# Attention and two MLPs on one core: four sequences per attention turn, and a planner that takes VectorE and GpSimd as excluding each other

## The chip, the cores and the metric

The kernel runs on one core of a Trainium2 chip. Its time is the device time of one execution in microseconds (us); the three timed runs of the kernel before gave 564.5, 564.63 and 563.31 us, median 564.5. The engines are named as the profile names them: PE (TensorE; PEld is its weight load), DVE (VectorE), ACT (ScalarE), POOL (GpSimd), SP (SyncE, which here issues every DMA).

## What is computed

Three layers stand one behind the other. The first is a linear attention with decay, in chunks of the sequence (4 sequences, 8 heads, 768 positions, head width 32, state width 16); the other two are MLPs over the 3072 rows of 256 values that it makes (inner width 2048).

```python
for c in range(nc):                                   # chunks, in order
    cum = np.cumsum(la, axis=-1)                      # la = log of the decay a
    L = np.exp(cum[..., :, None] - cum[..., None, :]) * causal
    M = np.einsum('bhin,bhjn->bhij', Cc, Bc) * L
    y_intra = np.einsum('bhij,bhjd->bhid', M, xc)
    y_inter = np.einsum('bhin,bhnd->bhid', Cc, state) * np.exp(cum)[..., None]
    y[:, :, sl] = y_intra + y_inter
    state = decay_full * state + np.sum(Bx, axis=2)   # Bx: B and x, decayed to the chunk's end
x = softplus(y_rows @ w_in) @ w_out                   # first MLP
x = g2(x @ w2_in) @ w2_out                            # second MLP; g2 is 0, a square, or the value itself
```

## The kernel before

**Work units.** A chunk is 128 positions, so there are NC = 6 chunks of four sequences (NB = 4), and a *unit* u is one sequence in one chunk (u = 4c + b). The 512 columns of a chunk (4 sequences by 128 positions) are what the MLPs take at a time. An MLP *step* is one slice of 128 inner values for one chunk: `up` (6 matmuls of 512 columns into a PSUM bank `h`, L1262 to L1264), the activation on ACT, its split into a rounded half `g_hi` and a rest `g_lo`, and `down` (6 matmuls into the chunk's two accumulators `acc`, L1398). Each MLP has 16 steps a chunk. Later chunks and the second MLP form pairs of chunks in products with fewer multiplications (L1269 to L1271). At the start some steps are cut: a half step has 256 columns (two sequences) and two slices. The first `WHOLE` steps take `down` in one product of full precision (L1386) in place of three rounded ones, and so need no rounded weights of the second kind.

**Attention.** Chunk 0 goes unit by unit. From chunk 1 on a *pair* of units goes through three PE jobs, each with MLP steps between: `scores` (L1104), the products of B and C, into four PSUM banks (the pair `y` and two of the four `acc`); `st` (L1172, L1150), half of the intra-chunk product and the new states into `y`; and `out` (L1204, L1172), the rest. Between `scores` and `st` DVE multiplies the scores by the decays (`weigh`, L1118, into `ld`); between `st` and `out` it updates the state (`carry`, L1160) and ACT masks it (`sm`, L1241). Behind `out` ACT takes the sums out of PSUM (`evac`) and DVE makes the rest (`ready`, L1232). The decays of a pair come from DRAM into one of two `ld` buffers (`rows`, L1039; DVE then scans them, L1069), x, B and C into one of four `u` buffers (L1028); both are given back by `out`.

**Order.** `program` lists all jobs with their needs, engines, costs and buffers, and `Jobs.order` (L47) simulates the engines with these costs and picks the next job by due time. The order so found is written out engine by engine, and each engine keeps to it. Where a DVE and a POOL job overlap, the planner lengthens both by factors from the table `SHARED` (L495); `RUSH` (L526) moves single due times; jobs with two engines in braces go to the one that ends first by the plan. Where the plan leaves PE idle in the first 26 us, matmuls without use (`idle`, L1477) are put in.

Of the kernel before, what the change touches and what calls it, by code (L numbers as in the profile page):

```python
# [27 lines left out]
class Jobs:  # L28
# [18 lines left out]
    def order(self, slots, begin):  # L47
# [33 lines left out]
        busy = {DVE: [], POOL: []}  # L81
# [19 lines left out]
        for _ in range(len(jobs)):  # L101
            best = []
            for name in ready:
# [11 lines left out]
                (b for b in best if b[4] == first[4] and b[0] <= first[0] + (PATIENCE if first[0] > EARLY else HASTE)), key=lambda b: (b[1], b[0], b[2])  # L115
# [8 lines left out]
            if engine in (DVE, POOL):  # L124

                kind = name if isinstance(name, str) else name[0]
                other = POOL if engine == DVE else DVE
                for a, b, k in busy[other][-3:]:
                    shared = max(0.0, min(b, start + cost) - max(a, start))
                    cost += shared * SHARED[engine].get(kind, 0.0) * (k > 0)  # L130
                    if b == clock[other]:
                        clock[other] += shared * k * (SHARED[engine].get(kind, 0.0) > 0)
                busy[engine].append((start, start + cost, SHARED[engine].get(kind, 0.0)))
# [63 lines left out]

def pair_of(u):

    return u | 1  # L200
# [12 lines left out]
def program():  # L213
# [27 lines left out]
    for hg in range(2):  # L241
        add(("columns", hg), DVE, 610, needs=["terms"] + [("rows_of", 0)] * hg)
    for b in range(NB):
        add(("rows_of", b), DVE, 210, needs=["terms"] + [("columns", 1), ("rows_of", b - 1)] * (b == NB - 1), gives=["terms"] * (b == NB - 1))
# [7 lines left out]
    for u in range(NU):  # L252
# [18 lines left out]
        if c == 0:  # L271
            for hg in range(2):
                add(
                    ("sources", u, hg), POOL, 400, takes=["bt"] * (hg == 0),
                    needs=[("load", u), ("decay", u, hg)] + ([("sources", u, 0)] if hg else []),
                )
        else:
            add(("sources", u), DVE, 210, needs=[("load", u)] + decay, takes=["bt"])
        if b % 2:
            v = u // 2  # L280
            add(
                ("scores", v), PE, 830 if c else 1270, needs=[("load_bc", v)] + (decay + [("decay", u - 1)] if c else [("scores", v - 1)] * v),
                takes=["y", "y", "acc", "acc"] if c else ["y", "y"] + [("acc", "h")] * 2 if v == 0 else [("h", "acc")] * 4,
                gives=[("load_bc", v)],
            )
        for hg in range(2):
# [3 lines left out]
            bank = [("part", ("scores", u // 2), b % 2 * 2 + hg)]  # L290
            if n in WEIGH_POOL:
                add(("copy", u, hg), ACT, 490, needs=[("scores", u // 2)], takes=["g"], gives=bank)
                add(("weigh", u, hg), POOL, 1350, needs=weighed + [("copy", u, hg)], gives=[("copy", u, hg)])
            else:
                add(("weigh", u, hg), DVE, 340 if c else 600, needs=weighed + [("weigh", u, 0)] * hg + [("scores", u // 2)], gives=bank)
        both = [u] if c == 0 else [u - 1, u]
        if c == 0 or b % 2:

            needs = [("weigh", i, hg) for i in both for hg in range(2)] + ([("out", both[0] - 1)] if u else [])
            if c > 0:  # L300
                add(
                    ("st", u), PE, 990, needs=needs + [("sm", u - NB)], takes=["y", "y"], gives=[("sources", i) for i in both],
                )
                add(("carry", u), DVE, 300, needs=[("st", u), ("dec", c)])
                add(("sm", u, 1), ACT, 500, needs=[("carry", u)])
                needs = [("st", u), ("sm", u, 1)] + [("cd", i) for i in both]
# [5 lines left out]
            needs = [("out", u)]  # L312
# [3 lines left out]
            if c == 1:  # L316

                needs += [("w2" if signed(0, kind, SX) else "w3", 0, kind, SX) for kind in "io"]
            due = when(first_step[c, b] - LEAD if c < 2 else min(first_step[c, b] - LEAD, CHUNK * (c - 1) + SPACE * b + SHIFT))
# [3 lines left out]
                gives=[("st", u) if c else ("out", u)] + [("dec", c)] * (b == NB - 1 and c > 0),  # L323
# [13 lines left out]
    for m in range(2):  # L337
        for j in sorted(range(8), key=lambda j: first_use[m, j]):
            for kind in "io":
# [20 lines left out]
                if m == 0:  # L360
                    add(("split_w", *w), {DVE: 610, POOL: 1500}, needs=[("w_hi", *w)])
# [44 lines left out]
    for s, (m, c, t0, n, fc, m_fc) in enumerate(steps):  # L406
# [47 lines left out]
        else:  # L454
            add(("g_hi", s), {ACT: 520, DVE: 360}, needs=[("g", s)], takes=["gh"])
            add(("g_lo", s), {DVE: 610, POOL: 1500} if s < GL_POOL else {DVE: 610}, needs=[("g_hi", s)], takes=["gl"], gives=[("g", s)])
# [8 lines left out]
        if s == same[-1]:  # L465
            root = ("down", same[0])
            for e in range(2):
                own = when(s) + LAG + 2000 if m else None
                add(("finish_hi", s, e), {ACT: 490, DVE: 610}, due=own, needs=[("down", s)],
                    takes=[("w32", "cs")] * (m + (s == len(steps) - 1 and e)), gives=[("part", root, e)] * m)  # L470
# [7 lines left out]
    slots = dict(sx=2, h=2, y=2, z=0, acc=4, t=2, g=N_G, gh=4, gl=3, ld=3, lp=2, u=4, bc=3, bt=3, dec=2, st=2, st2=1, st3=1, w32=5, cs=2)  # L478
# [1052 lines left out]
```

## Time and profile before

| what | value |
|---|---|
| timed runs | 564.5, 564.63, 563.31 us (median 564.5) |
| the profiled execution: its own time | 563.84 us |
| its span in the profile | 561.9 us |
| time outside the span | 1.94 us |
| PE busy | 553.3 us, 98% |
| DVE, ACT, POOL busy | 449.9, 385.1, 27.6 us |
| granted TensorE clock, mean | 0.998 |

The profile gives each instruction's start and duration. A matmul of 512 columns is recorded as some 0.39 us long, but the next one starts after some 0.23 us, since they are pipelined; how long a step of PE takes is therefore read from start to start. Within a view of instructions in order of time equal neighbours are merged (x32), and a bracket tells the idle time ahead and what ended it.

### The profile page before, as it was taken

To read this page: it belongs to the slowest core of one execution; us is meant where nothing else is said; L and a number is where in the kernel's file an instruction comes from. 1 tells how busy PE (TensorE), PEld (TensorE's weight loads), DVE (VectorE), ACT (ScalarE), POOL (GpSimd) and SP (SyncE) were. 2 spreads that over 40 slices of the span, in tenths; PEclk is the share of its full clock that TensorE was granted. 3 is DMA by queue.
4 is the path that set the end of the run, shared out by engine and by line. 5 is a ranking of instruction groups with operands and counts; after the bars stand their busy time and mean duration, and the time that the engine had idled before them with its cause. 6 is when DMAs were issued, how large, how long until landed. Compare 5 with 4: busy or idle time off the path is not lost.

```text
span 561.9 us, 10574 instructions
## 1 busy us (share of the span) xinstructions
PE 553.3 (98%) x4070; PEld 445.4 (79%) x4070; DVE 449.9 (80%) x841; ACT 385.1 (69%) x706; POOL 27.6 (5%) x34
## 2 busy tenths in 40 slices
PE   9899999999999999999999999999999999999997
PEld 4767898777778888788888788788788888888885
DVE  6899976687896899877897999967976665876664
ACT  6977744445555666756657887886787785777873
POOL 4030300000000100000100000200100000000000
PEclk9999999999999999999999999999999999999999
DMA  8986541658445003578847132103200001000002
GB/s 283 389 225 187 157 118 31 196 171 225 119 149 178 0 2 93 214 237 304 275 142 240 59 118 90 56 6 108 76 0 1 0 1 38 37 1 0 1 1 76
DMA packets 34679, 64.74 MB, mean 115 GB/s; under 512 B 3684, under 2 KB 8164, under 8 KB 34628
## 3 DMA queue, kind: packets, MB, share of 16 engines
q1 hardware_dynamic: 34628, 64.06, 35.3%
q8 instruction: 32, 0.52, 0.4%
q14 instruction: 19, 0.16, 0.1%
HBM read 47.61 MB, written 16.43 MB: 114 GB/s over the span
## 4 chain that ended last, share of the span: by engine, by line
PE 91%; DVE 4%; DMA 2%; ACT 1%; SPq 1%; issue 1%; DVEq 0%; ACTq 0%
PE acc L1398 44%; PE h L1262 5%; PE h L1269 4%; PE h L1263 4%; PE h L1264 4%; PE h L1271 4%; PE h L1270 4%; PE z L1269 4%; PE z L1271 4%; PE z L1270 4%; PE y L1172 2%; DMA st<-in_w_out_dram 2%; PE acc L1386 1%; PE y L1204 1%; PE y L1104 1%
## 5 line engine op out<-in xcount | busy, mean ns | idle before, releaser
L1372 DVE TENSOR_TENSOR gl<-g,gh 128x512 fp32r<-128x512 f32 x184 | 126.5, 692 | 51.3 <-PE acc L1398 35.4
L1398 PE MATMUL acc<-gh,woh 128*128 128x512 f32 (+1 forms) x384 | 148.9, 390 | 0.0
L1398 PE MATMUL acc<-gh,wol 128*128 128x512 f32 (+1 forms) x384 | 146.5, 384 | 0.0
L683 ACT CAST gh<-g 128x512 fp32r<-128x512 f32 x155 | 96.1, 620 | 32.2 <-PE acc L1398 18.4
L1398 PE MATMUL acc<-gl,woh 128*128 128x512 f32 (+1 forms) x384 | 115.1, 383 | 0.0
L1398 PEld LDWEIGHTS acc<-gh,woh 128*128 128x128 f32 x384 | 72.1, 188 | 16.1 <-issue 1.2
L1398 PEld LDWEIGHTS acc<-gh,wol 128*128 128x128 f32 x384 | 72.2, 188 | 13.5 <-DVE wol L916 0.2
L1398 PEld LDWEIGHTS acc<-gl,woh 128*128 128x128 f32 x384 | 70.9, 188 | 14.4
L1357 ACT ACTIVATE g<-h 128x512 f32<-128x512 f32 x65 | 38.7, 595 | 56.2 <-PE h L1264 41.3
L1349 ACT ACTIVATE t<-t 128x512 f32<-128x512 f32 x96 | 60.8, 634 | 1.9
L1262 PE MATMUL h<-xh,wih 128*128 128x512 f32 (+1 forms) x130 | 48.5, 373 | 0.0
L1263 PE MATMUL h<-xh,wil 128*128 128x512 f32 (+1 forms) x130 | 46.6, 358 | 0.7 <-DVE wil L916 0.7
L1264 PE MATMUL h<-xl,wih 128*128 128x512 f32 (+1 forms) x130 | 46.3, 356 | 0.0
L1263 PEld LDWEIGHTS h<-xh,wil 128*128 128x128 f32 x130 | 24.5, 189 | 4.8 <-DVE wil L916 1.1
L1069 DVE TENSOR_TENSOR_SCAN ld<-ld,eye_t 128x512 f32<-128x512 f32 x20 | 25.8, 1326 | 3.2 <-DMA ld<-clip_z 3.2
L1262 PEld LDWEIGHTS h<-xh,wih 128*128 128x128 f32 x130 | 24.5, 189 | 4.5 <-issue 0.4
L1264 PEld LDWEIGHTS h<-xl,wih 128*128 128x128 f32 x130 | 24.5, 189 | 3.6
L1342 ACT ACTIVATE t<-h 128x512 f32<-128x512 f32 x37 | 22.1, 597 | 7.6 <-PE h L1271 6.0
L1361 DVE TENSOR_TENSOR g<-h,t 128x512 f32<-128x512 f32 x37 | 25.3, 684 | 1.8 <-ACT t L1349 0.8
L1361 DVE TENSOR_TENSOR g<-z,t 128x512 f32<-128x512 f32 x35 | 23.8, 683 | 1.5 <-ACT t L1349 0.8
L1342 ACT ACTIVATE t<-z 128x512 f32<-128x512 f32 x35 | 20.9, 596 | 5.5 <-PE z L1271 3.2
L1322 DVE TENSOR_TENSOR dec_plain<-h,dec_plain 128x512 f32<-128x512 f32 x22 | 15.1, 688 | 7.8 <-PE h L1271 7.6
(321 smaller groups left out, 1004.2 us busy)
## 6 DMA issues: line engine op xcount, KB each, us to landing
st<-in_w_in_dram SPq DMA_DIRECT2D x15, 512.0 KB, 4.0
st<-in_w_out_dram SPq DMA_DIRECT2D x15, 512.0 KB, 4.2
u<-in_ub_dram SPq DMA_DIRECT2D x24, 256.0 KB, 5.5
ld<-clip_z SPq DMA_DIRECT2D x20, 256.0 KB, 4.6
bc<-in_bc_dram SPq DMA_DIRECT2D x12, 384.0 KB, 7.9
pre_i<-st_plain SPq DMA_DIRECT2D x14, 256.0 KB, 3.6
pre_o<-st_plain SPq DMA_DIRECT2D x12, 256.0 KB, 3.7
pre_s<-st_plain SPq DMA_DIRECT2D x14, 192.0 KB, 4.0
```

The source lines that it names most:

```text
L683: nc.scalar.copy(out, in_)
L1262: nc.tensor.matmul(o, wh, xh[c][:, k, t0:t0 + n], start=(k == 0), stop=False)
L1263: nc.tensor.matmul(o, wl, xh[c][:, k, t0:t0 + n], start=False, stop=False)
L1264: nc.tensor.matmul(o, wh, xl[c][:, k, t0:t0 + n], start=False, stop=(k == 1))
L1269: nc.tensor.matmul(bank, wh, bh, start=start, stop=False, skip_group_check=True)
L1270: nc.tensor.matmul(bank, wl, bh, start=False, stop=False, skip_group_check=True)
L1271: nc.tensor.matmul(bank, wh, bl, start=False, stop=True, skip_group_check=True)
L1342: nc.scalar.activation(out=t, in_=ph, func=act_funcs.IDENTITY_SAT240, scale=SAT)
L1349: nc.scalar.activation(out=t, in_=t, func=AF.Square, scale=0.5 / SAT, bias=0.5)
L1361: nc.vector.tensor_tensor(out=g, in0=ph, in1=t, op=ALU.max)
L1372: engines[engine].tensor_tensor(out=mine("g_lo", s)[0], in0=mine("g", s)[0], in1=mine("g_hi", s)[0].bitcast(F32), op=ALU.subtract)
L1398: nc.tensor.matmul(acc_t(s, e), w, g[:, j * n:(j + 1) * n], start=(begins(e, j) and g is gh and i == 0), stop=(fc + j == NFC - 1 and g is ...
```

## The change

Four things change. (1) In chunks 1 to 5 (`TOGETHER`) the three PE jobs each take all four units; the states then go to two `acc` banks, the four units' sums fill the pair `y`, the first two units' scores stand in the first half of a bank and the others' in the second, and `u`, `ld` and `bt` are given back by one `out` for all. (2) The planner: a POOL job starts where no DVE job of the set `LOCKED` runs, and such a DVE job waits for the end of a POOL job that has begun; constants and due times differ, `SHARED` is gone and `RUSH` is short; chunk 1 has no half steps, and 8 steps, not 6, take the full-precision `down`. (3) `rows_of`, four products that fill the rows of exponents for chunk 0, may run on ACT. (4) Of the last result, which two engines copy out in halves, ACT issues the first half's transfer.

```diff
-            if engine in (DVE, POOL):
-
-                kind = name if isinstance(name, str) else name[0]
-                other = POOL if engine == DVE else DVE
-                for a, b, k in busy[other][-3:]:
...
+            kind = name if isinstance(name, str) else name[0]
+            if engine == POOL:
+
+                begun = start + 60
+                for a, b in locked:
+                    if a < begun + cost and b > begun:
+                        begun = b
+                shared = [name, begun, begun + cost]
+                cost += begun - start
+            elif engine == DVE and kind in LOCKED:
+                if shared and start < shared[2] and start + cost > shared[1]:
+                    if start <= shared[1]:
...
+                    else:
+                        cost += shared[2] - start
+                locked = locked[-20:] + [(start, start + cost)]
...
+def units_of(u):
+
+    c = u // NB
+    return [u] if c == 0 else list(range(NB * c, NB * c + NB)) if c in TOGETHER else [u - 1, u]
...
+        if u == both[-1] and b % 2:
             v = u // 2
+            pairs = [v - 1, v] if n_pairs == 2 else [v]
             add(
-                ("scores", v), PE, 830 if c else 1270, needs=[("load_bc", v)] + (decay + [("decay", u - 1)] if c else [("scores", v - 1)] * v),
+                ("scores", v), PE, 200 + 630 * n_pairs if c else 1270,
+                needs=[("load_bc", i) for i in pairs] + ([("decay", i) for i in both[:2]] if c else [("scores", v - 1)] * v),
...
+            seen = ("scores", last_of(u) // 2)
+            early = n_pairs == 2 and b < 2
+            bank = [("part", seen, b % 2 * 2 + hg)] * (not early)
...
+                before = [("weigh", u, 0)] * hg + [("weigh", u - 2, hg)] * (n_pairs == 2 and not early)
+                add(("weigh", u, hg), DVE, 340 if c else 600, needs=weighed + before + [seen], gives=bank)
...
             if c > 0:
                 add(
-                    ("st", u), PE, 990, needs=needs + [("sm", u - NB)], takes=["y", "y"], gives=[("sources", i) for i in both],
+                    ("st", u), PE, 200 + 790 * n_pairs, needs=needs + [("sm", i - NB) for i in both[1::2]],
+                    takes=["y", "y"] + ["acc", "acc"] * (n_pairs == 2), gives=[("sources", i) for i in both],
...
+                for i in both[1::2]:
+                    add(("carry", i), DVE, 300, needs=[("st", u), ("dec", c)])
+                    add(("sm", i, 1), ACT, 500, needs=[("carry", i)])
+                needs = [("st", u)] + [("sm", i, 1) for i in both[1::2]] + [("cd", i) for i in both]
...
-                ("out", u), PE, 1220 if c else 750, needs=needs, takes=["y"] * (c == 0),
-                gives=[("load", i) for i in both] + [("rows", u) if c else ("part", ("spread", u, 0), 1)]
+                ("out", u), PE, 200 + 1010 * n_pairs if c else 750, needs=needs, takes=["y"] * (c == 0),
+                gives=[("load", i) for i in both] + ([("rows", i) for i in both[1::2]] if c else [("part", ("spread", u, 0), 1)])
...
+        if c == 0 or b % 2:
+
+            end = last_of(u) if c else u
+            needs = [("out", end)]
...
+            if c and u == end and n_pairs == 2:
+                needs += [("ready", u - 2)]
...
-ORDER = [
-    (0, 0, 0, 4), (0, 1, 0, 4), (0, None, 4, 12), (1, 0, 0, 6), (1, 1, 0, 6), (1, None, 6, 10),
-]
-WHOLE = 6
+ORDER = [(0, 0, 0, 4), (0, 1, 0, 4), (0, None, 4, 12), (1, None, 0, 16)]
+WHOLE = 8
...
 }
+TOGETHER = (1, 2, 3, 4, 5)
+BT = 4
...
-PRE_FROM = 11
-BIAS = {DVE: 200, POOL: 2200}
+PRE_FROM = 3
+BIAS = {DVE: 400, POOL: 500}
...
-HASTE = 200
-CHUNK = 8
+HASTE = 0
+STAND_BY = 400
+FAR = 10000.0
+CHUNK = 9
...
-STRETCH = 1.02
+STRETCH = 1.0
...
 LAG = 1500
-LAG_1 = 6000
+LAG_1 = 9000
...
 RUSH = {
-    ("cd", 6): -2000, ("columns", 1): -2000, ("decay", 2, 1): 16000, ("down", 1): -1000, ("down", 11): -4000,
...
+    ("decay", 2, 1): -8000, ("decay", 5): -16000, ("load_w", 1, "i", 2): -16000, ("w3", 0, "o", 4): 8000,
 }
...
     def rows_of(engine, b):
         r = slice(64, 128)
-        nc.vector.tensor_scalar(
-            out=rows_t[r, b], in0=tiles["terms"][r].bitcast(F32), scalar1=of_seq[r, b:b + 1], scalar2=-1.0,
-            op0=ALU.mult, op1=ALU.mult,
-        )
+        terms = tiles["terms"][r].bitcast(F32)
+        if engine == ACT:
+            nc.scalar.activation(out=rows_t[r, b], in_=terms, func=AF.Copy, scale=less_seq[r, b:b + 1])
+        else:
+            nc.vector.tensor_scalar(out=rows_t[r, b], in0=terms, scalar1=less_seq[r, b:b + 1], scalar2=None, op0=ALU.mult)

     @job
...
-                nc.sync.dma_start(out[steps[s][1], e, :, i * n:i * n + n], part[:, 0:n])
+                queue = nc.scalar if len(parts_of) > 1 and i == 0 else nc.sync
+                queue.dma_start(out[steps[s][1], e, :, i * n:i * n + n], part[:, 0:n])
         else:
             nc.sync.dma_start(clip_z.rearrange("u s (h i) -> (u s) h i", h=H), z_t)
...
     def cb_t(u, hg):
-        return buf(*got["scores", u // 2][u % 2 * 2 + hg])
+        bank = buf(*got["scores", last_of(u) // 2][u % 2 * 2 + hg])
+        return bank[:, 256:512] if u // NB in TOGETHER and u % NB > 1 else bank

     @job
     def scores(engine, v):
+
...
         intra_turn(u, 0)
-        for i in range(2):
-            x, bt = parts(u - 1 + i)[0], flat(bt_t(u - 1 + i))
+        for i in units_of(u):
+            x, bt = parts(i)[0], flat(bt_t(i))
             for p in range(4):
                 for s in range(2):
                     r, o = slice(s * HALF, s * HALF + HALF), slice(p * 32, p * 32 + 32)
                     nc.tensor.matmul(
-                        states_t(u, s)[o, i], bt[r, p * 32:p * 32 + 32], x[r, p * 64:p * 64 + 64], start=False, stop=True,
-                        skip_group_check=True,
+                        states_t(i | 1, s)[o, i % 2], bt[r, p * 32:p * 32 + 32], x[r, p * 64:p * 64 + 64],
+                        start=u // NB in TOGETHER and i % NB == 0, stop=True, skip_group_check=True,
                     )

...
-        for i in (u - 1, u):
+        for i in units_of(u):
             for h in range(4):
                 for s in range(2):
-                    intra(i, (s + turn) % 2 * 4 + h, halves[s], halves[s], turn == 0 and i == u - 1)
+                    intra(i, (s + turn) % 2 * 4 + h, halves[s], halves[s], turn == 0 and i == units_of(u)[0])

     def out_unit(engine, u):
```

How the instructions move, at three places.

PE, `out` of chunk 1 (y: the sums; sm: masked states; ld: weighed scores; u: x, B and C). Before, the second pair's, with the matmul ahead of it and the one behind:

```order
L1264 MATMUL h_207<-xl_376,wih_79 128x512
L1204 MATMUL y<-u_131,sm_142 64x64 x4
L1204 MATMUL y<-u_131,sm_143 64x64 x4
L1204 MATMUL y<-u_132,sm_142 64x64 x4
L1204 MATMUL y<-u_132,sm_143 64x64 x4
L1172 MATMUL y<-ld_120,u_131 32x64 x8
L1172 MATMUL y<-ld_120,u_132 32x64 x8
L1398 MATMUL acc_282<-gh,woh_94 128x512
```

Now, all four units, with the matmul ahead:

```order
L1450 MATMUL acc_270<-gl,woh_95 128x512
L1255 MATMUL y<-u_130,sm_141 64x64 x4
L1255 MATMUL y<-u_130,sm_142 64x64 x4
L1255 MATMUL y<-u_131,sm_141 64x64 x4
L1255 MATMUL y<-u_131,sm_142 64x64 x4
L1255 MATMUL y<-u_132,sm_143 64x64 x4
L1255 MATMUL y<-u_132,sm_144 64x64 x4
L1255 MATMUL y<-u_133,sm_143 64x64 x4
L1255 MATMUL y<-u_133,sm_144 64x64 x4
L1223 MATMUL y<-ld_122,u_130 32x64 x8
L1223 MATMUL y<-ld_122,u_131 32x64 x8
L1223 MATMUL y<-ld_121,u_132 32x64 x8
```

The same matmuls stand in one run of twice the length (the last of the four `ld` rows follows); before there are two such runs a chunk, with MLP steps between.

SP, the loads for chunk 2, behind chunk 1's `out` (ld: decays; dec: decay of the state; bc: operands of the scores; st: staged MLP weights). Before:

```order
L1039 DMA ld_121<-clip_z 64x2x512 x2
L1028 DMA u_129<-in_ub_dram 128x512
L1028 DMA u_130<-in_ub_dram 128x512
L730 DMA st_137<-in_w_out_dram 128x2x512
L1023 DMA bc_242<-in_bc_dram 128x768
L1039 DMA ld_120<-clip_z 64x2x512 x2
L1028 DMA u_131<-in_ub_dram 128x512
L1028 DMA u_132<-in_ub_dram 128x512
L1046 DMA dec_133<-clip_p 128x1x512
```

Now:

```order
L769 DMA st_136<-in_w_in_dram 128x2x512
L1080 DMA ld_121<-clip_z 64x2x512 x2
L1080 DMA ld_122<-clip_z 64x2x512 x2
L1069 DMA u_130<-in_ub_dram 128x512
L1069 DMA u_131<-in_ub_dram 128x512
L1069 DMA u_132<-in_ub_dram 128x512
L1069 DMA u_133<-in_ub_dram 128x512
L1087 DMA dec_134<-clip_p 128x1x512
L769 DMA st_137<-in_w_in_dram 128x2x512
```

Before, a pair's decays and its two units come together and another pair's follow; now the decays of both pairs stand ahead of the four units, and a load of MLP weights ahead of them all.

DVE, chunk 2, `weigh` (L1118 before, L1166 now) and the scans of the decays (those with eye_t). Before, the first pair's `weigh` and the second pair's scans:

```order
L685 CAST woh_96<-w_855 128x512
L1118 TENSOR_TENSOR ld_121<-y,ld_121 128x256
L1118 TENSOR_TENSOR ld_121<-acc_286,ld_121 128x256
L1118 TENSOR_TENSOR ld_121<-y,ld_121 128x256
L1118 TENSOR_TENSOR ld_121<-acc_268,ld_121 128x256
L1069 SCALAR_TENSOR_TENSOR ld_120<-ld_120,eye_t 128x512 x2
L1160 SCALAR_TENSOR_TENSOR s_66<-s_66,dec_134,y 128x64 x2
L1077 TENSOR_TENSOR bt_304<-u_131,ld_120 128x128
L1077 TENSOR_TENSOR bt_298<-u_132,ld_120 128x128
L1089 TENSOR_TENSOR u_131<-u_131,dec_134 128x128
```

Now, from the scans on:

```order
L1110 SCALAR_TENSOR_TENSOR ld_121<-ld_121,eye_t 128x512 x2
L1110 SCALAR_TENSOR_TENSOR ld_122<-ld_122,eye_t 128x512 x2
L1118 TENSOR_TENSOR bt_301<-u_130,ld_121 128x128
L1118 TENSOR_TENSOR bt_306<-u_131,ld_121 128x128
L1166 TENSOR_TENSOR ld_121<-y,ld_121 128x256
L1166 TENSOR_TENSOR ld_121<-acc_268,ld_121 128x256
L1118 TENSOR_TENSOR bt_323<-u_132,ld_122 128x128
L1118 TENSOR_TENSOR bt_357<-u_133,ld_122 128x128
L1166 TENSOR_TENSOR ld_121<-y,ld_121 128x256
L1166 TENSOR_TENSOR ld_121<-acc_291,ld_121 128x256
L1166 TENSOR_TENSOR ld_122<-y,ld_122 128x256
L1166 TENSOR_TENSOR ld_122<-acc_268,ld_122 128x256
```

Before, a pair's `weigh` stands ahead of the next pair's scans, and a `carry` (L1160) behind them; now all four scans of a chunk come first, and its eight `weigh` (two more follow) in one stretch.

## Rows read from the trace of the kernel before

**Rows 1.** The page: span, and each engine's busy time, share and instructions.

```profile
span 561.9 us, 10574 instructions
...
PE 553.3 (98%) x4070; PEld 445.4 (79%) x4070; DVE 449.9 (80%) x841; ACT 385.1 (69%) x706; POOL 27.6 (5%) x34
```

**Rows 2.** Two stretches (us): length; PE, PEld, DVE, ACT, POOL busy; clock, DMA share, GB/s.

```profile
60.00:173.00 113.00, 113.00 (x1790) 89.73 (x1790) 90.19 (x201) 59.43 (x119) 1.32 (x2) 1.00 0.49 145
173.00:562.00 389.00, 383.94 (x1686) 315.44 (x1684) 305.90 (x540) 279.64 (x500) 10.02 (x7) 1.00 0.25 82
```

**Rows 3.** PE in order of time, 190 us (start, us, instruction): one step's `up`.

```profile
190.44 0.39 PE L1262 MATMUL z<-xh,wih 128*128 128x512 f32 x1
...
191.80 0.39 PE L1398 MATMUL acc<-gh,woh 128*128 128x512 f32 x1
```

**Rows 4.** The same view, 104 to 116 us: one pair's attention between steps.

```profile
104.31 0.50 PE L1398 MATMUL acc<-gh,woh 128*128 128x512 f32 x1
...
107.26 0.45 PE L1172 MATMUL y<-ld,u 64*32 64x64 f32 x32
...
108.05 0.50 PE L1398 MATMUL acc<-gh,woh 128*128 128x512 f32 x1
...
110.99 0.69 PE L1204 MATMUL y<-u,sm 32*64 32x64 f32 x32
...
112.00 0.50 PE L1398 MATMUL acc<-gh,woh 128*128 128x512 f32 x1
...
114.99 0.34 PE L1104 MATMUL y<-bc 32*64 32x128 f32 x4
...
115.28 0.29 PE L1104 MATMUL acc<-bc 32*64 32x128 f32 x4
...
115.39 0.29 PE L1104 MATMUL acc<-bc 32*64 32x128 f32 x4
115.61 0.50 PE L1398 MATMUL acc<-gh,woh 128*128 128x512 f32 x1
```

**Rows 5.** The same view, 79 to 83 us: a half step's `up` and a `down`.

```profile
79.55 0.28 PE L1262 MATMUL h<-xh,wih 128*128 128x256 f32 x1
...
82.37 0.28 PE L1262 MATMUL h<-xh,wih 128*128 128x256 f32 x1
```

**Rows 6.** The same view, 37 to 40 us: a `down` of full precision.

```profile
37.74 1.88 PE L1386 MATMUL acc<-gh,w 128*128 128x512 f32 x4
39.55 0.34 PE L1104 MATMUL y<-bc 32*64 32x128 f32 x4
```

**Rows 7.** What PE waited for: us in total, times, longest.

```profile
PE y L1477 <- DVE xl L1232: 1.8, 1, 1.8
...
PE h L1263 <- DVE wil L916: 0.7, 1, 0.7
```

**Rows 8.** ACT in order of time: the first activation of the MLP.

```profile
20.67 0.60 ACT L1357 ACTIVATE gh<-h 128x512 f32<-128x512 f32 x1
```

**Rows 9.** DMA issues of SP in order of time, 76 to 80 us.

```profile
76.81 1.73 SPq L1039 DMA_DIRECT2D ld<-clip_z  x2
```

**Rows 10.** DVE in order of time: a pair's scans, and one `weigh`.

```profile
82.18 2.34 DVE L1069 TENSOR_TENSOR_SCAN ld<-ld,eye_t 128x512 f32<-128x512 f32 x2 [1.67 <-DMA ld<-clip_z]
...
93.04 0.42 DVE L1118 TENSOR_TENSOR ld<-y,ld 128x256 f32<-128x256 f32 x1
```

**Rows 11.** DVE in order of time: the last copy.

```profile
558.27 0.42 DVE L685 COPY st_plain<-acc 128x256 f32<-128x256 f32 x1 [1.07 <-ACT st_plain L683]
```

**Rows 12.** DVE in order of time, 27 to 32 us: two casts.

```profile
27.50 1.39 DVE L685 CAST wih<-w 128x512 fp32r<-128x512 f32 x1
...
31.21 0.43 DVE L685 CAST wih<-w 128x512 fp32r<-128x512 f32 x1
```

**Rows 13.** POOL in order of time, 27 us.

```profile
27.07 2.96 POOL L916 TENSOR_TENSOR wol<-w,woh 128x512 fp32r<-128x512 f32 x2 [12.91 <-ACT woh L683]
```

More of the change, by code (lines that the diff above doesn't have):

```diff
@@ L80, in order @@
         held = {}
-        busy = {DVE: [], POOL: []}
+        locked, shared = [], None
         self.start, self.end, self.done = {}, {}, {}
@@ L123, in order @@
             cost += SIGNAL * (engine == DVE)
-            if engine in (DVE, POOL):
-                kind = name if isinstance(name, str) else name[0]
-                other = POOL if engine == DVE else DVE
-                for a, b, k in busy[other][-3:]:
[L129 to L133, printed above, removed]
+            kind = name if isinstance(name, str) else name[0]
[9 more added lines that the diff above has]
+                    if start <= shared[1]:
+                        late = start + cost - shared[1]
+                        shared[1] += late
+                        shared[2] += late
+                        clock[POOL] = self.done[shared[0]] = shared[2]
+                        self.end[shared[0]] += late
+                        for other in after[shared[0]]:
+                            if other in at:
+                                for e in at[other]:
+                                    at[other][e] = max(at[other][e], shared[2] + (80 if e == POOL else self.LATENCY[POOL]))
+                    else:
+                        cost += shared[2] - start
+                locked = locked[-20:] + [(start, start + cost)]
             clock[engine] = start + cost
@@ L241, in program @@
     for hg in range(2):
-        add(("columns", hg), DVE, 610, needs=["terms"] + [("rows_of", 0)] * hg)
+        add(("columns", hg), DVE, 610, needs=["terms"] + [("columns", 0)] * hg)
     for b in range(NB):
-        add(("rows_of", b), DVE, 210, needs=["terms"] + [("columns", 1), ("rows_of", b - 1)] * (b == NB - 1), gives=["terms"] * (b == NB - 1))
+        add(("rows_of", b), {DVE: 210, ACT: 200}, needs=["terms"] + [("columns", 1), ("rows_of", b - 1)] * (b == NB - 1), gives=["terms"] * (b == NB - 1))
     add("clip_load", SP, 400, due=-1e5, size=98e3)
@@ L322, in program @@
                 ("ready", u), DVE, 610 + 300 * (c < NC - 1) if c else 340, due=due, needs=[("evac", u)],
-                gives=[("st", u) if c else ("out", u)] + [("dec", c)] * (b == NB - 1 and c > 0),
+                gives=([("st", u)] * (u == end) if c else [("out", u)]) + [("dec", c)] * (b == NB - 1 and c > 0),
             )
@@ L360, in program @@
                 if m == 0:
-                    add(("split_w", *w), {DVE: 610, POOL: 1500}, needs=[("w_hi", *w)])
+                    add(("split_w", *w), {DVE: 610, POOL: 1300}, needs=[("w_hi", *w)])
                     continue
@@ L455, in program @@
             add(("g_hi", s), {ACT: 520, DVE: 360}, needs=[("g", s)], takes=["gh"])
-            add(("g_lo", s), {DVE: 610, POOL: 1500} if s < GL_POOL else {DVE: 610}, needs=[("g_hi", s)], takes=["gl"], gives=[("g", s)])
+            add(("g_lo", s), {DVE: 610, POOL: 1300} if s < GL_POOL else {DVE: 610}, needs=[("g_hi", s)], takes=["gl"], gives=[("g", s)])
             needs = [("g_lo", s)] + before + [("split_w", m, "o", j) for j in pieces]
@@ L469, in program @@
                 add(("finish_hi", s, e), {ACT: 490, DVE: 610}, due=own, needs=[("down", s)],
-                    takes=[("w32", "cs")] * (m + (s == len(steps) - 1 and e)), gives=[("part", root, e)] * m)
+                    takes=[("w32", "cs")] * m + [("cs",)] * (s == len(steps) - 1 and e), gives=[("part", root, e)] * m)
                 if m == 0:
@@ L587, in join @@
     def join():
-        assert jobs.start["out", NB - 1] < jobs.start["scores", NB // 2]
+        assert len(of_pair) == 1
         for i in range(2):
@@ L1214, in columns_of @@
         n, o = (Q, b * Q) if c == 0 else (2 * Q, b * Q - Q)
[L1215 removed]
+        first = o if c in TOGETHER else 0
+        y = y_t(b)[0] if c == 0 else bufs["pair"][:, :, first:first + n]
         return [y] + [t[c][:, :, o:o + n] for t in (xh, xl)]
```

55 lines of the change are left out of this document (29 added, 26 removed).

## The prediction

> **What bounds the kernel now.** Read the page's head first. PE is busy for 553.3 of 561.9 us, and DVE, the next engine, for 449.9 [rows 1]. The windows say the same by stage: from 60 to 173 us PE has no idle time at all, and from 173 to 562 us it is idle for 389.00 - 383.94 = 5.1 us, while DVE idles there for 389.00 - 305.90 = 83 us and POOL is hardly used, 10.02 us in 7 instructions [rows 2]. The granted clock is 1.00 of full speed in both. So the end is set by how long PE takes for its list of matmuls, and a change moves the time by what it takes off that list or what it makes PE wait for. What PE waited for is small and lies at the start: 1.8 us on the first `xl`, once, and 0.7 us on a rest of weights [rows 7].
>
> The next view is PE in order of time, since a busy PE need not be an efficient one. I call the six matmuls of 512 columns of an `up` or of a `down` a run. Among equal neighbours a run takes 191.80 - 190.44 = 1.36 us from start to start [rows 3]. In the attention of chunks 1 to 5 the same runs take longer: between the first block (ended at 104.31) and the second (107.26) there are two in 2.95 us, between second and third (108.05 to 110.99) two in 2.94, and behind the third (112.00 to 114.99) two in 2.99 [rows 4], against 2.72. So each block costs its neighbours about 0.24 us, beside its own length of 0.79 (`st`), 1.01 (`out`) and 0.62 us (`scores`) [rows 4]. Each block also has an end of its own: the last group of `scores` started 0.11 us behind the one before, but the matmul behind it came only 0.22 us later [rows 4], 0.11 more. An edge between attention and MLP therefore costs some 0.24 + 0.11 = 0.35 us a block.
>
> **The change part by part.** *Blocks.* Before, chunks 1 to 5 have two pairs with three blocks each, 30 blocks. Now they have 15, and in the written-out order each is a single run of twice the length (the fence on `out`); the number of attention and MLP matmuls is the same. So 15 edges go: 15 x 0.35 = -5.3 us. From below, only the 0.24 us that the neighbours show goes: -3.6. From above, a block's beginning costs inside it what its end does, 0.24 + 2 x 0.11 = 0.46: -6.9. I take 0.35, which rows show. That the blocks gain nothing is excluded by the same rows: a run is slow only beside another shape, and 15 of these places go.
>
> *Half steps.* Chunk 1's are gone. Half an `up` and the `down` behind it take 82.37 - 79.55 = 2.82 us for as many columns as two runs of 2.72 [rows 5], 0.10 more. The written-out order holds ten such pairs before and four now: 6 x 0.10 = -0.6 us (between 0 and -1.2, if the other neighbour pays as much).
>
> *`WHOLE` 8.* A `down` of full precision takes 39.55 - 37.74 = 1.81 us ahead of a block [rows 6], where a run with an edge behind it takes about 1.36 + 0.12 = 1.48. Two more of them: 2 x 0.34 = +0.7 us. That two slices need no rounded output weights takes work off DVE and POOL at the start; I count that as nothing, since PE waits there only for the 0.7 us of [rows 7].
>
> *Start.* `rows_of` may go to ACT: four small products, each below the 0.60 us of a whole activation [rows 8]. They stand ahead of the first activation, which before begins at 20.67 us. What hides them is POOL's work on `bt`, for which DVE waits anyway; if that cover were gone, 4 x 0.60 = +2.4 us. From the other side, the order of the first units is planned anew, and both waits of [rows 7] could go: -1.8 - 0.7 = -2.5. Nothing in the trace says which end is nearer; the first `up` needs the same loads and products. I take 0.
>
> *Loads of the next chunk.* One `out` now gives back all `ld` and `u`, so a chunk's loads can't start while the other pair is still to be computed. Queued behind it on SP are both pairs' decays, then the units, with a weight load ahead (the fence on SP). Before, the issue of a pair's decays is at 76.81 us and takes 1.73 [rows 9], and the scan that waits for it starts at 82.18 [rows 10], 5.37 us behind the issue. Now the chain from the end of `out` to the end of the last `weigh` is: some 0.2 to the issue, 1.73 for the first pair's issue, 5.37 for the second's way, 2.34 for its scans, 0.5 for `bt` (two of about the 0.3 us by which one `weigh` follows the next, less their overlap), and eight `weigh` in one stretch (the fence on DVE), each 0.42 us long [rows 10] and, as they overlap like the scans, some 0.34 apart, 2.7: 12.8 us. Queued behind the waiting scan on DVE are `g_lo` splits, and `down` would wait for them. Against this PE has, in the new order, ten runs and the doubled `scores` from `out` to the next `st` in chunks 2 and 3: 10 x 1.36 + (2 x 0.62 - 0.11) + two edges of 0.24 = 15.2 us; in chunks 4 and 5 it has twelve and fourteen runs. So 2.4 us are to spare, the cover is PE's own work, and I count +0.3 us for a `g_lo` that comes late here or there (between 0 and +3, which is a late load of 3.9 us in two chunks).
>
> *Tail.* The last copy on DVE starts at 558.27 after waiting 1.07 us for ACT's half [rows 11]. The transfer that sets the end is that of this later half, which stays on SP. Moving the first half to ACT's queue saves at most its issue on SP, which the wait hides: 0 (between -1 and +0.5; +0.5 if ACT's issue delays what else ACT has to do).
>
> *Planner.* DVE and POOL jobs are kept apart by plan; no instruction of the chip waits for that, it is only an order. But POOL's list grows: behind the start it has 17 instructions of 128x512 where it had 7, each about 10.02 / 7 = 1.43 us [rows 2]. What two such instructions do to DVE shows at 27 us: a cast took 1.39 us [rows 12] while POOL computed from 27.07 for 2.96 us [rows 13]; the next cast of the same form took 0.43 [rows 12]. So one overlap cost DVE 0.96 us. Ten more are at worst 10 us, of DVE's 83 idle ones. Counted at nothing here, and as a rival below.
>
> A rule of the Trainium skill bears on this (SBUF — State Buffer, section "Who interferes with whom"): VectorE in a two-port mode, or with two operands from SBUF, and GpSimd exclude each other, and the one that starts second waits for the whole instruction of the first. The cast of 1.39 us agrees with it. By the rule alone, each of the 17 jobs may stop DVE for its full 1.43 us, 24 us of the 83, and the sum stays as it is as long as none falls where PE waits for DVE.
>
> The sum: -5.3 - 0.6 + 0.7 + 0 + 0.3 + 0 = -4.9 us. The profiled execution took 563.84 us, 1.94 more than its span; 563.84 - 4.9 = 558.9, which I round to 559.0. The median of the runs shown, 564.5, is 0.66 above that execution, which is inside their own spread; it widens the range and doesn't move the forecast.
>
> **The rivals.** *A, GpSimd takes DVE's time where PE waits.* The ten more POOL jobs each hold DVE for the 0.96 us of [rows 12], and half of them fall on a split that PE waits for at once: 5 x 0.96 = +4.8, and 558.9 + 4.8 = 563.7, no change. For it: these jobs make operands of the next MLP or chunk (`xl`, `u_later`), which PE needs soon. Against it: 83 idle us of DVE [rows 2], and the plan has these instructions keep clear of each other.
>
> *B, the loads come late: slower.* The place is `st` of chunks 2, 3 and 4, the price what the chain above is longer than PE's way. It decides from a lateness of the decays of about 5.8 us: 2 x (5.8 - 2.4) + (5.8 - 2.4 - 2.7) = 7.5, hence 566.4. At 7 us it is 2 x 4.6 + 1.9 = 11.1, hence 570. For it: DMA engines are 0.49 busy at 145 GB/s from 60 to 173 us [rows 2], a weight load stands ahead in the queue, and the scan before already waited 1.67 us for its decays [rows 10]. Against it: before, the same queue with the same weight loads brought the decays in 5.37 us.
>
> *C, the edges don't shrink as far.* Only the neighbours' 0.24 us goes, and the start loses up to 1.5 of its bound of 2.4: 558.9 + 1.7 = 560.6, or 562.1 with both. For it: what lies inside a block can't be seen from one matmul's start; against it: the 0.22 us at its end.
>
> *D, more than forecast.* The edge is worth 0.46 and the waits of [rows 7] go: 558.9 - 1.6 - 2.5 = 554.8. For it: the start is planned anew; against it: the first `up` still waits for loads.
>
> **How the numbers follow.** The forecast as summed, from 556 to 561 us, has 0.62; C above 561 has 0.13, D below 556 has 0.10, A 0.09, B 0.06. What a measurement can tell from no change is 0.3%, 1.7 us: below 562.8 is faster, above 566.2 slower. Faster is the forecast, C and D, 0.85; the same is A, 0.09; slower is B, 0.06. The range leaves out B, A's worse half and D's far end: 555.5 to 563.0; the bounds of the blocks and the start fill it.
>
> **What would show it.** Right: PE's blocks of attention come 15 times in chunks 1 to 5, with runs of about 1.48 us beside them and of 1.36 elsewhere, the last matmul about 5 us earlier against the first, PE's waits together no more than now, and the scan of the next chunk's decays over well ahead of `st`. Wrong: `scores`, `st` or `out` of twice the length take more than twice the time; PE waits on `ld` at `st` (B), on `g_lo` or `xl` with DVE instructions above 1 us (A); or the first activation comes later than 20.67 us by more than 1 us (start).

## The result, and the profile after

Five runs of the changed kernel took 556.56 to 558.4 us, median 557.5; the kernel before 563.76 (five runs). The ratio is 0.9886, interval [0.9866, 0.9906]: 6.3 us faster, where 4.9 were forecast and 559.0 named. The profiled execution took 557.88 us. The page of the changed kernel gives the span and each engine's busy time, share and instructions; the rows of before are [rows 1].

```profile
span 556.2 us, 10449 instructions
...
PE 546.8 (98%) x3994; PEld 442.3 (80%) x3994; DVE 435.7 (78%) x813; ACT 391.7 (70%) x720; POOL 39.2 (7%) x45
```

The span is 5.7 us shorter, and the time outside it 0.3 (557.88 - 556.2 = 1.68 for 1.94), so this execution is 6.0 us shorter than the profiled one of before. To see where, the span is cut where the first product of a pair of chunks starts on PE: ahead of it stand the start and the attention of all chunks with the same MLP work in both kernels, behind it MLP steps alone. The windows of before (length first, then busy time and instructions of PE, PEld, DVE, ACT and POOL, granted clock, DMA share, GB/s):

```profile
0.00:225.80 225.80, 222.20 (x2619) 173.68 (x2620) 189.97 (x400) 138.71 (x273) 20.25 (x29) 1.00 0.51 159
225.80:561.90 336.10, 331.14 (x1453) 271.73 (x1451) 259.97 (x441) 246.36 (x434) 7.32 (x5) 1.00 0.25 86
```

and of after:

```profile
0.00:222.10 222.10, 216.97 (x2542) 170.16 (x2543) 185.88 (x395) 139.62 (x276) 20.52 (x30) 1.00 0.53 170
222.10:556.20 334.10, 329.86 (x1453) 272.14 (x1451) 249.80 (x419) 252.12 (x445) 18.72 (x15) 1.00 0.24 81
```

The first part is 3.7 us shorter and the second 2.0, at a clock of 1.00 in all four. The first holds the 15 blocks. PE in order of time (start, us, instruction), chunk 3 of the changed kernel, from its `scores` on:

```profile
93.99 0.34 PE L1152 MATMUL y<-bc 32*64 32x128 f32 x4
...
95.13 0.50 PE L1450 MATMUL acc<-gh,woh 128*128 128x512 f32 x1
...
96.62 0.39 PE L1314 MATMUL h<-xh,wih 128*128 128x512 f32 x1
...
100.79 0.80 PE L1223 MATMUL y<-ld,u 64*32 64x64 f32 x60
...
102.20 0.50 PE L1450 MATMUL acc<-gh,woh 128*128 128x512 f32 x1
...
103.70 0.39 PE L1314 MATMUL h<-xh,wih 128*128 128x512 f32 x1
...
105.15 1.16 PE L1255 MATMUL y<-u,sm 32*64 32x64 f32 x64
106.24 0.88 PE L1223 MATMUL y<-ld,u 64*32 64x64 f32 x64
107.05 0.50 PE L1450 MATMUL acc<-gh,woh 128*128 128x512 f32 x1
```

The run behind a block takes 96.62 - 95.13 = 1.49 us and 103.70 - 102.20 = 1.50, as beside the shorter blocks in [rows 4]. The blocks themselves are shorter than two of before: `st` 102.20 - 100.79 = 1.41 for 2 x 0.79, `out` 107.05 - 105.15 = 1.90 for 2 x 1.01, and `scores` 95.13 - 93.99 = 1.14 for 2 x 0.62. That is 0.39 a chunk, 2.0 in five, and with 15 x 0.24 beside the blocks 5.6 us.

What PE waited for, in the changed kernel (us in total, times, longest):

```profile
PE acc L1438 <- ACT gh L1409: 2.1, 2, 1.5
...
PE y L1223 <- DVE ld L1166: 0.8, 1, 0.8
PE h L1315 <- DVE wil L955: 0.7, 1, 0.7
PE h L1314 <- ACT wih L722: 0.5, 1, 0.5
```

Together 4.1 us where [rows 7] has 2.5: the first wait (once 1.5 for the first activation) replaces the 1.8 on `xl`, and 0.6 on a later activation, 0.8 on `ld` at `st` of chunk 2 and 0.5 on a rounded weight are new. So the first part gains 5.6 us in blocks and gives back 1.6 in waits, 4.0 where 3.7 are seen; 0.3 us stays unnamed. In the second part PE's waits before are small ones that VectorE and ACT end, such as

```profile
PE h L1269 <- DVE h L1312: 0.3, 1, 0.3
PE z L1269 <- ACT h L1297: 0.3, 1, 0.3
```

The list of waits misses most of them, since a matmul is recorded as 0.39 us long and the next can start 0.227 us behind it. Summed over PE's rows from start to start, the intervals above 0.26 us exceed the usual 0.227 by 2.5 us before (13 of them) and by 0.6 after (4). That is 1.9 of the 2.0.

### The profile page after: what moved, and what is told of

It is laid out like the page before. It is cut to its first block, busy times and chain, and to the rows that moved or that the text cites. A ratio compares the mean times of both kernels' runs of the same rounds, so it can differ in the third digit from the quotient of the medians.

```text
span 556.2 us, 10449 instructions
## 1 busy us (share of the span) xinstructions
PE 546.8 (98%) x3994; PEld 442.3 (80%) x3994; DVE 435.7 (78%) x813; ACT 391.7 (70%) x720; POOL 39.2 (7%) x45
## 4 chain that ended last, share of the span: by engine, by line
PE 87%; DMA 8%; DVE 2%; ACT 1%; SPq 1%; issue 1%; DVEq 0%; ACTq 0%
PE acc L1450 44%; PE h L1321 5%; PE h L1323 5%; PE h L1322 5%; PE z L1321 4%; PE z L1323 4%; PE z L1322 4%; PE h L1314 3%; PE h L1315 3%; PE h L1316 3%; DMA raw<-in_w_out_dram 2%; DMA ld<-clip_z 2%; DMA dec<-clip_p 2%; PE y L1223 1%; DMA st<-in_w_out_dram 1%; DMA u<-in_ub_dram 1%
## 5 line engine op out<-in xcount | busy, mean ns | idle before, releaser
L1450 PE MATMUL acc<-gh,woh 128*128 128x512 f32 x368 | 144.3, 392 | 0.0
L1450 PE MATMUL acc<-gh,wol 128*128 128x512 f32 x368 | 143.3, 389 | 0.0
L722 ACT CAST gh<-g 128x512 fp32r<-128x512 f32 x172 | 106.8, 621 | 26.4 <-PE acc L1450 14.2
L1450 PE MATMUL acc<-gl,woh 128*128 128x512 f32 x368 | 113.6, 389 | 0.0
L1450 PEld LDWEIGHTS acc<-gh,wol 128*128 128x128 f32 x368 | 69.1, 188 | 14.1
L1315 PE MATMUL h<-xh,wil 128*128 128x512 f32 (+1 forms) x114 | 42.9, 376 | 0.7 <-DVE wil L955 0.7
L1316 PE MATMUL h<-xl,wih 128*128 128x512 f32 (+1 forms) x114 | 42.9, 376 | 0.0
L1314 PEld LDWEIGHTS h<-xh,wih 128*128 128x128 f32 x114 | 21.4, 188 | 6.2 <-issue 1.1
L1316 PEld LDWEIGHTS h<-xl,wih 128*128 128x128 f32 x114 | 21.4, 188 | 4.0
L1409 ACT ACTIVATE g<-z 128x512 f32<-128x512 f32 x19 | 11.4, 598 | 17.4 <-PE z L1316 8.8
```

The source lines that it names most:

```text
L722: nc.scalar.copy(out, in_)
L1314: nc.tensor.matmul(o, wh, xh[c][:, k, t0:t0 + n], start=(k == 0), stop=False)
L1315: nc.tensor.matmul(o, wl, xh[c][:, k, t0:t0 + n], start=False, stop=False)
L1316: nc.tensor.matmul(o, wh, xl[c][:, k, t0:t0 + n], start=False, stop=(k == 1))
L1409: nc.scalar.activation(out=g, in_=ph, func=AF.Softplus)
L1450: nc.tensor.matmul(acc_t(s, e), w, g[:, j * n:(j + 1) * n], start=(begins(e, j) and g is gh and i == 0), stop=(fc + j == NFC - 1 and g is ...
```

## The experiments

All are the changed kernel with one edit. Where a kernel was planned anew, its whole order may move; "order kept" means that only the named instructions did.

**pairs.** Attention in pairs, planned anew.

```
-TOGETHER = (1, 2, 3, 4, 5)
+TOGETHER = ()
```

> The changed kernel with TOGETHER empty: attention in pairs again, 30 blocks on PE in chunks 1 to 5, and all else of the change kept (planner, no half steps in chunk 1, 8 whole steps, rows_of, the last transfer). Theory 1 (the gain is PE's edges between attention and MLP, about 0.37 us for each of 15 blocks, of which 0.24 beside the block and 0.13 inside it): 5.5 us slower than the changed kernel, so about 563, ratio to the kernel before 0.998. Theory 2 (the gain comes from the new order of the start and of VectorE and GpSimd): stays at 557 to 559, ratio 0.988 to 0.992.

Measured 568.46 us, 1.0092 [1.0077, 1.0107]: 11 us above the changed kernel, twice what theory 1 gives; theory 2 falls. The 30 blocks are there, but so are new waits of PE:

```profile
PE acc L1450 <- DVE gl L1424: 1.6, 2, 1.2
...
PE acc L1450 <- ACT gh L722: 1.3, 1, 1.3
...
PE y L1223 <- DVE s L1211: 0.8, 1, 0.8
```

Planned anew, this kernel isn't one part less: its plan is worse than that of the kernel before as well. So it shows that the other parts, planned in this way, don't give the gain, and it can't size the edges.

**split.** Each block as two halves, with a delay in the planner that puts a run between; planned anew.

```
+HALVES = {"scores_b": "scores", "st_b": "st", "out_b": "out"}
-  max(at[other][e], done + 80 if e == engine != SP else end)
+  max(at[other][e], done + (1250 if other[0] in HALVES else 80) if e == engine != SP else end)
```

> The changed kernel with each scores, st and out of four units written as two halves of two units, with a run of six MLP matmuls between (29 blocks in place of 15; one st stays whole); buffers, loads and planner are for four units as in the changed kernel, and the matmuls are the same. Theory 1 (edges): 14 x 0.37 = 5.2 us slower than the changed kernel, about 562.7. Theory 2 (the start and the planner): no slower, 557 to 558.5. Theory 3 (the gain lies in having one set of waits and loads per chunk, not in the shape changes on PE): also 557 to 558.5.

Measured 564.26 us, 1.0007 [0.9993, 1.0021]: 6.8 us slower than the changed kernel, theory 1 and somewhat more. It speaks against theories 2 and 3, but this kernel too is planned anew, and in its trace PE waits 1.6 us on `xl`, which the changed kernel doesn't; so by itself it doesn't part the edges from the plan.

**three.** `TOGETHER = (3, 4, 5)`, planned anew.

> The changed kernel with only chunks 3, 4 and 5 together and chunks 1 and 2 in pairs: 21 blocks. Theory 1: 6 x 0.37 = 2.2 us slower than the changed kernel, about 559.7. Theory 2: as the changed kernel, 557.5. If the gain came from chunks 1 and 2 alone, where PE waits for loads and splits are found, it would be near 563.

Measured 565.01 us, 1.0021 [1.0007, 1.0035], 7.5 us slower for six blocks. As with pairs, this plan has brought waits of PE in chunks 1 and 2 (1.2 us on `gl`, twice 0.8 on the state `s`). None of the three expectations holds; the run tells nothing on the edges.

**halves15 and halves5.** Order kept; each block (or only `out`) is cut in two and the next run of PE is put between the halves.

```
+  step = order.pop(k)          # PE's next job behind block i
+  order[k:k] = [step, ((name[0] + "_b", name[1]), PE, slots)]
```

> The changed kernel with its written-out order kept, except that each of the 15 blocks is cut in two halves of two units, with the next run of six MLP matmuls between them: 30 blocks, no other instruction moved. Theory 1 (edges on PE, 0.37 us a block): 15 x 0.37 = 5.5 us slower than the changed kernel, about 563, whatever DVE and POOL do. Theory 2 (most of the gain is in the new order of VectorE, GpSimd and the loads): less than 2 us slower, below 559.5. The run split, with a plan of its own, left open whether its 6 us were edges or plan.

> As halves15, but only the five out blocks are cut: 20 blocks. Theory 1: a third of it, 5 x 0.36 = 1.8 us slower than the changed kernel, about 559.3. Theory 2: no difference that can be measured. If what costs is the later end of out (loads of the next chunk start 1.4 us later, and PE waits 0.98 us for ld in chunk 2), the wait at st grows by 1.4 us in chunk 2 and there alone.

halves15 measured 564.29 us, 1.0014 [0.9997, 1.0032], by the ratios 7.2 us above the changed kernel (by the medians 6.8); halves5 560.27, 0.9946 [0.9925, 0.9967], 3.4 above (2.8), each give or take some 1.6. Theory 2 falls: with the new order kept and the long blocks cut, no gain over the kernel before can be measured. PE in order of time in halves15, a cut `out`:

```profile
110.72 0.69 PE L1292 MATMUL y<-u,sm 32*64 32x64 f32 x32
111.34 0.45 PE L1255 MATMUL y<-ld,u 64*32 64x64 f32 x32
111.72 0.50 PE L1487 MATMUL acc<-gh,woh 128*128 128x512 f32 x1
...
113.32 0.69 PE L1292 MATMUL y<-u,sm 32*64 32x64 f32 x32
113.95 0.45 PE L1255 MATMUL y<-ld,u 64*32 64x64 f32 x32
114.33 0.50 PE L1351 MATMUL h<-xh,wih 128*128 128x512 f32 x1
```

The halves are 111.72 - 110.72 = 1.00 and 1.01 us long again, and the run between them takes 113.32 - 111.72 = 1.60: two edges of 0.12 on one run. That is 0.24 + 0.13 a cut, 5.6 us for 15. The rest is waits, as PE's rows of halves15 show:

```profile
PE y L1183 <- DMA bc<-in_bc_dram: 2.4, 1, 2.4
PE acc L1475 <- ACT gh L1446: 1.5, 1, 1.5
...
PE y L1255 <- DVE ld L1192: 0.9, 1, 0.9
PE acc L1487 <- DVE xl L1508: 0.8, 1, 0.8
```

The 0.8 on `xl` falls inside a cut `out` of chunk 2; with it the sum is 6.4, within the interval. The 2.4 on `bc` is a late load at the very start of the profiled execution, which took 566.38 us, 2.1 above this kernel's median; behind it three of the changed kernel's waits, 1.8 us, are missing. The dose of a third (1.9 us by the same sum, and 0.6 more wait on `ld`, not the 1.4 of the last expectation) fits halves5.

**gl_dve.** `GL_POOL = 0`: no `g_lo` on GpSimd, planned anew.

> The changed kernel with all g_lo on VectorE (GL_POOL 0). In the changed kernel two g_lo of GpSimd (69.42 to 72.87 us) lie beside the four scans of chunk 2, which take 6.16 us where four scans elsewhere take about 4.7, and PE then waits 0.98 us (from start to start) for ld at st. If GpSimd's hold on the shared port makes that wait, the scans take about 4.7 us here, the wait at that st is gone and the kernel is 0.5 to 1 us faster, about 556.7, unless the three g_lo on VectorE (0.6 each) stand ahead of the scans. If the wait comes from late loads, the scans' start is what counts and the time stays at 557.5.

Measured 588.2 us, 1.0429 [1.0407, 1.0452]. The new plan lets the first products' operands come late, far from the place in question:

```profile
PE h L1321 <- ACT xh L722: 13.6, 1, 13.6
```

So it tells nothing on that place. The windows around this wait, which lasts from 229.44 to 243.04 us (columns as above), and two matmuls that follow each other behind it:

```profile
225.00:240.00 15.00, 4.44 (x20) 3.35 (x18) 10.54 (x28) 5.42 (x13) 0.00 (x0) 0.73 0.44 161
240.00:243.00 3.00, 0.00 (x0) 0.00 (x0) 2.62 (x5) 0.62 (x1) 0.00 (x0) 0.50 0.07 25
...
256.00:262.00 6.00, 6.00 (x21) 4.75 (x20) 3.39 (x6) 3.67 (x8) 0.00 (x0) 0.73 0.17 46
262.00:280.00 18.00, 18.00 (x81) 14.91 (x80) 13.50 (x27) 11.32 (x20) 0.00 (x0) 1.00 0.57 182
```

```profile
249.30 0.63 PE L1322 MATMUL h<-xh,wil 128*128 128x512 f32 x1
249.73 0.63 PE L1323 MATMUL h<-xl,wih 128*128 128x512 f32 x1
```

**rest_zero.** Order kept; the two `g_lo` at 69 to 73 us are left out, with a fill of zeros in their place.

```
+        if engine == POOL and s in (14, 15):
+            nc.gpsimd.memset(mine("g_lo", s)[0].bitcast(F32), 0.0)
+            return
```

> The changed kernel, order kept, with the two g_lo of GpSimd at 69 to 73 us replaced by a fill with zeros on GpSimd, which reads nothing (the rest of the two activations is left out). The four scans of chunk 2 took 6.16 us beside these two. If GpSimd's reads hold DVE up, the scans take about 4.7 us here and the wait of 0.98 us for ld at st goes: 0.5 to 1 us faster than the changed kernel. If a scan is as long beside any GpSimd work, or if the scans are long for another reason, they stay at 6.2 us, and the time at 557.5.

Measured 556.43 us, 0.9868 [0.9847, 0.9889]. This is the place in the changed kernel, VectorE and then GpSimd in order of time, and the scans in one row (ns: shortest, median, longest):

```profile
70.02 6.16 DVE L1110 TENSOR_TENSOR_SCAN ld<-ld,eye_t 128x512 f32<-128x512 f32 x4 [1.42 <-DMA ld<-clip_z]
```

```profile
69.42 3.45 POOL L1424 TENSOR_TENSOR gl<-g,gh 128x512 fp32r<-128x512 f32 x2 [11.01 <-ACT gh L722]
```

```profile
L1110 DVE TENSOR_TENSOR_SCAN ld<-ld,eye_t x4: 1192/1484/2233, 70.0 to 75.0; 128x512 f32<-128x512 f32 x4
```

and the same scans on VectorE without the two:

```profile
71.11 4.57 DVE L1110 TENSOR_TENSOR_SCAN ld<-ld,eye_t 128x512 f32<-128x512 f32 x4 [1.63 <-DMA dec<-clip_p]
```

6.16 us became 4.57, and PE's wait at this `st` is gone, although the scans start 1.1 us later (0.6 of it because `out` of chunk 1 ends later in this execution, 63.82 us for 63.27). So it was GpSimd that made the scans long, and without it the loads leave no wait. The fills ended ahead of the scans, so whether one that only writes would hold them up isn't shown. In time the 1.0 us can't be told from nothing.

**late_pin.** Order kept; the 17 late GpSimd jobs on VectorE (12 `t_lo`) and ACT (5 `t_hi`).

```
-            emit[kind](engine, *args)
+            emit[kind]({"t_hi": ACT, "t_lo": DVE}.get(kind, engine), *args)
```

> The changed kernel, order kept, with the late GpSimd work taken off it: the rests (t_lo) of the operands of the products on VectorE, the rounded halves (t_hi) on ACT, 17 instructions in all. Rival A (GpSimd's jobs hold VectorE up where PE waits, 0.96 us each): 1 to 5 us faster. Theory 1 (the idle 83 us of VectorE take them): within 1 us of the changed kernel.

Measured 557.95 us, 0.9901 [0.9884, 0.9918]: within 1 us, so GpSimd's late work costs nothing here that can be measured. Nor does it make most of the second part's gain: by the sum from start to start the second part here exceeds the usual by 1.2 us, so 1.3 of the 1.9 stays. VectorE takes the work almost for nothing. The changed kernel's window and this run's (columns as above):

```profile
173.00:556.00 383.00, 378.95 (x1670) 312.81 (x1668) 292.16 (x513) 283.74 (x506) 21.27 (x17) 1.00 0.24 80
173.00:556.00 383.00, 379.57 (x1672) 313.06 (x1670) 293.69 (x526) 285.35 (x511) 0.00 (x0) 1.00 0.24 80
```

VectorE is busy for only 1.5 us more, although it does 12 more subtractions of some 0.69 us. In the changed kernel its own instructions took longer beside GpSimd's, such as this pair, VectorE and GpSimd:

```profile
190.22 1.78 DVE L902 TENSOR_TENSOR st_plain<-st_plain 128x512 f32<-128x512 f32 x1
```

```profile
189.84 1.62 POOL L927 TENSOR_TENSOR xl<-st_plain,xh 128x512 fp32r<-128x512 f32 x1
```

There 8 of VectorE's 370 instructions of this shape behind 173 us took more than 0.9 us, here none. So the planner's order doesn't keep the two engines apart on the chip, and GpSimd's 21.27 us took 1.5 us off VectorE and 1.6 off ScalarE.

**better.** Order kept; the two `g_lo` on VectorE, one ahead of the scans, where it waits, the other between `weigh`.

```
+        move(("decay", 8), ("decay", 9))
+        move(("g_lo", 14), ("decay", 8))
+        move(("g_lo", 15), ("up", 18))
```

> The changed kernel, order kept, with the two g_lo of GpSimd at 69 to 73 us moved to VectorE: one ahead of the four scans of chunk 2, where VectorE waits 1.4 us for the loads, the other between the first two and the next six weigh. If GpSimd's work beside the scans cost the wait at st: the scans take about 4.6 us in place of 6.16, the weigh end about 1 us earlier, the wait of 0.98 us at st is gone and the time is 0.5 to 1 us below the changed kernel's, 556.5 to 557, with the reference's result kept. If only the work itself counts, VectorE has 1.2 us more and the wait grows.

Measured 557.8 us, 0.9892 [0.9874, 0.9909]: no faster. The place does what was expected, VectorE and then PE in order of time:

```profile
70.20 0.69 DVE L1424 TENSOR_TENSOR gl<-g,gh 128x512 fp32r<-128x512 f32 x1 [0.80 <-ACT gh L722]
70.81 4.56 DVE L1110 TENSOR_TENSOR_SCAN ld<-ld,eye_t 128x512 f32<-128x512 f32 x4
```

```profile
79.37 0.39 PE L1316 MATMUL h<-xl,wih 128*128 128x512 f32 x1
79.69 0.48 PE L1223 MATMUL y<-ld,u 64*32 64x64 f32 x33
```

`st` follows without a wait. But in the profiled execution the loads of `ld` were issued 1.2 us later than in the changed kernel's. SP there, and here:

```profile
63.35 3.02 SPq L1080 DMA_DIRECT2D ld<-clip_z  x4
```

```profile
64.59 3.50 SPq L1080 DMA_DIRECT2D ld<-clip_z  x4
```

One cause is a longer wait of PE at the start than the 0.5 us above:

```profile
PE h L1314 <- ACT wih L722: 1.1, 1, 1.1
```

What the start varies by covers the gain. No version that beats the changed kernel is shown.

**rows_dve and old_start.** The first has parts 3 and 4 undone, order kept; the second has the old `ORDER` and `WHOLE = 6`, planned anew.

> The changed kernel, order kept, with parts 3 and 4 undone: the four rows_of on VectorE and both halves of the last result issued by SP. The prediction's steps give 0 for each (bounds -2.5 to +2.4 and -1 to +0.5): within 0.5 us of the changed kernel. If ACT's rows_of had brought the start forward, the first up comes later and the time is up to 1 us longer.

> The changed kernel planned with the old list of first steps (half steps in chunk 1 again) and 6 steps of full precision. By the prediction's terms: 6 x 0.10 more for the half steps and 0.7 less for two whole downs, so within 0.5 us of the changed kernel, if the plan is otherwise as good; every wait that the new plan adds or loses comes on top, and the trace must tell it apart. If the gain over the kernel before were in the start, the time would go back by several us.

rows_dve measured 557.1 us, 0.9892 [0.987, 0.9913]: nothing. old_start 559.37, 0.9932 [0.991, 0.9955], 1.9 to 2.6 slower. Its windows, cut at the first product:

```profile
0.00:222.40 222.40, 216.48 (x2618) 174.75 (x2619) 187.97 (x402) 139.24 (x274) 23.46 (x32) 1.00 0.53 170
222.40:558.00 335.60, 330.48 (x1453) 272.05 (x1452) 249.60 (x413) 255.05 (x450) 16.52 (x14) 1.00 0.24 81
```

The part with the half steps is 0.3 us longer than in the changed kernel, where the two terms give 0.1 shorter. The rest, 1.4 us, comes behind it, where PE has the same matmuls (one wait of 0.9 us on `z` is most of it): again the plan.

## Why the prediction was right

*Blocks.* Right, by its own rows: 5.3 forecast, 5.6 in the trace of the changed kernel, and 5.6 in that of halves15, where the long blocks are cut with the order kept and the time rises by 7.2, give or take 1.6. The two shares were sized from one end and its neighbours, 0.24 and 0.11; they are 0.24 and 0.13.

*Half steps, `WHOLE`, `rows_of`, tail.* -0.6 + 0.7 + 0 + 0: old_start's first part bears out the sum of the first two within 0.4 us, though neither alone, rows_dve the others within what can be measured.

*Start and added waits.* The sizes were wrong and cancelled, which is luck. PE's first wait changed its place (from 1.8 on `xl` to 1.5 on the first activation), near the 0 that the forecast took without a row for it; but 1.6 us of waits came in the first part where +0.3 was named. Two of the prediction's own signs failed with it: PE's waits together are no longer 2.5 us but 4.1, and PE waits on `ld` at `st`. The 2.0 us that go in the second part were no term at all: the prediction put every late wait of PE down as staying. That is the step that was missing, and the main reason why 6.0 to 6.3 came and not 4.9. Which constant of the planner took these waits away isn't shown; late_pin shows only that it is for the most part not GpSimd's work, and old_start that a small edit to the list of steps brings 1.4 back.

*Rival B (late loads)* came only in part, at its place: PE waits for `ld` in chunk 2. The chain had 9.6 us from the end of `out` to the end of the scans, with the first pair's scans done while the second pair's loads were on their way. Instead the first scan starts 70.02 - 63.35 = 6.7 us behind the issue and all four follow in one row, to 76.18, 12.9 us behind `out` with the 0.1 to the issue: 3.3 us more, of which GpSimd makes 1.6. The other 1.7 alone fits into the slack of 2.4; both together left the wait of 0.8.

*Rival A* was right as a mechanism, wrong in its place: GpSimd's 17 late jobs hold VectorE up as well, but not where PE waits for it; PE waited once, behind the scans at 70 us. A rule of the Trainium skill (SBUF — State Buffer, section "Who interferes with whom") says that a VectorE instruction with two operands from SBUF, as these scans have with `ld` and `eye_t`, contends with a GpSimd instruction that reads SBUF, and that the lock is exclusive. The trace agrees. GpSimd's two `g_lo` end at 69.42 + 3.45 = 72.87 us. The first two scans, in a row of their own

```profile
70.02 3.93 DVE L1110 TENSOR_TENSOR_SCAN ld<-ld,eye_t 128x512 f32<-128x512 f32 x2 [1.42 <-DMA ld<-clip_z]
```

end at 70.02 + 3.93 = 73.95, 1.08 us later, which is a scan's pace (4.57 / 4 = 1.14): the second scan, the one of 2.23 us, did its work when GpSimd had ended.

## What to carry to other kernels

Where one engine is busy throughout, price its changes of shape from start to start beside the block and inside it, and count how many go: that term held to 0.3 us in the two traces where it could be read by itself. Terms worth 1 to 2 us in the waits of the other stages come with any new plan; give them a range with both signs, and test a part with the order kept, since a part undone and planned anew (pairs, three, gl_dve) measures the plan. Before work is moved from VectorE to GpSimd, ask what the other engines gain: here it was 1.5 us on VectorE and 1.6 on ScalarE for 21 us of GpSimd's time.

## What the runs showed of the hardware

In gl_dve the granted clock of TensorE fell while PE stood still for 13.6 us: its mean is 0.73 from 225 to 240 us and 0.50 of full speed, the lower of its two levels, from 240 us on. It was 1.00 again from 262 us, when PE had been busy throughout since 256. In between two matmuls follow each other by 249.73 - 249.30 = 0.43 us in place of 0.23. So the operand that came 13.6 us late cost PE its clock as well, and that is part of the 31 us by which this kernel is longer than the changed one.
